# Wider weights, grouped transposes, reordered loads and new priorities in a fused attention and feed-forward kernel

## The chip, the cores and the metric

The kernel runs on one core of one Trainium2 chip. The time is the device time of that core in microseconds (us), lower is better. Each kernel was run several times; a "fast" run is one within 1.5% of the fastest of the same kernel. Engines: PE is TensorE's matmul side, PEld its weight loads, DVE is VectorE, ACT is ScalarE, POOL is GpSimd, SP issues most DMAs.

## The reference, cut to what matters

The input x has 2048 tokens of 448 values. The output is x plus two branches that share one layer norm.

```python
xn = layernorm(x)                                   # S = 2048, D = 448
# branch A: 16 heads of 28; pq = q @ w_phi, pk = k @ w_phi per head
phi_q = concat(softmax(pq), softmax(-pq))           # phi_k likewise: 56 features a head
kv  = einsum("bhsf,bhsd->bhfd", phi_k, v);  z = sum over s of phi_k
o   = einsum(phi_q, kv) / (einsum(phi_q, z) + 1e-6)
A   = o @ wo
# branch B: F = 1792
B   = silu(xn @ w1) @ w2
out = x + A + B
```

All inputs are bf16. 448 is 3.5 times 128, so every product over D has three full blocks of 128 rows and a remainder of 64.

## The kernel before: the parts that matter here

The program is written as a list of operations with their reads and writes. A planner inside the kernel simulates them with estimated durations and so fixes the order of each engine's instructions before anything runs. On the chip each engine then runs its list in that order and waits on semaphores. So an estimate or a priority changes only the order; but a wrong place in the order can stall an engine that has other ready work behind it.

```python
def transpose(dst, src, idn, name):                 # one planned operation for each transpose
    P.op("pe", 56.0, lambda e: e.transpose(dst, src, idn), ...)

def ln_tile(t):                                     # 128 tokens
    ...                                             # DVE statistics, POOL (var + eps) ** -0.5
    P.op("dve", 390, ... xn = (x - mean) * rstd)    # columns 0:448
    P.op("dve", 170, ... xn_sb[:, sl, D:512] = xn_sb[:, sl, KF:D])   # remainder again, KF = 384
    tps = bank16[7][:, 0:512]...                    # one PSUM bank for all x transposes
    for kt in range(4):
        transpose(tps[:, kt, :], xn_sb[:, sl, kt * 128:(kt + 1) * 128], ident[:], "xnT_tr")
    copy(dstx, tps, 512, "xnT_ev")                  # DVE; tiles 8 to 15 are transposed by DMA instead
```

The first layer of branch B (w1, then Silu) works on chunks of 512 tokens, so chunk 1 needs the transposed tiles 4 to 7. `fold` multiplies w_phi into wq and wk: eight weight transposes, an ACT copy, eight small matmuls and a copy, four times.

The attention stage takes 16 tiles; DVE sums, POOL normalises and TensorE accumulates kv:

```python
def kv(t):
    for c in range(CC):                             # CC = 8, KP = 112, DA = 29
        mm(banks[5][0:KP, c*2*DA:(c+1)*2*DA], E_sb[:, sl, 1, c*KP:(c+1)*KP],   # weights 128 x 112
           vaug[:, t % NV, 2*c:2*c+2, :]..., ...)                              # 58 moving columns
```

The second layer of branch B (w2) is TensorE's filler. For the first eight tiles it is kept in SBUF as Y; for the others it stays in PSUM and wo is added to it:

```python
P.cur_prio = 3                                      # larger number: later choice
for t in range(NYT): y_tile(t, [6, 7][t % 2])       # NYT = 8, PSUM banks 6 and 7
...                                                 # order of outputs: 8, 0, 9, 1, ...
b = OUT_BANKS[ob_cnt[0] % 4]                        # 6, 7, 4, 5
q = att(t)                                          # U matmuls, divide, transpose, ACT copy; NQ = 3 buffers
if t < NYT: finish_tile(t, q, b, Y_sb[:, t, :], True)
else:
    P.cur_prio = 2
    ffn2(t, b, False)                               # filler
    P.cur_prio = 0
    finish_tile(t, q, b, x_sb[:, t, :], False)      # wo matmuls, DVE add, store
```

The softmax here doesn't subtract the row's maximum and nothing guards it: scores larger than these inputs give would overflow.

## Time and profile before

| kernel | median us | range | runs |
|---|---|---|---|
| before, with the prediction | 172.46 | 171.56 to 172.88 | 3 |

How to read the numbers below. "Busy" of PE counts from the start of a matmul to its modelled end, so overlapping matmuls hide how much time each really takes. The Trainium skill says so ("Trainium Kernel Development and Optimization", Performance Expectations: matmul busy time "is a bad metric for how close a kernel is to roofline, because matmuls are pipelined"); eight kv matmuls below are busy for 0.55 us but hold PE for 0.39 us. I therefore also use the *slot* of a matmul: the time from its start to the start of the next one, worked out from the trace. In this kernel the usual slot is 216 ns for 512 moving columns, 189 ns for 448 and 56 ns for a 128x128 transpose. Time above the usual slot is a wait of TensorE, but for one thing: the trace has 1170 matmul records for 1176 weight loads, and the slots of double length that the missing records leave are not counted as waits.

From the page of the kernel before: busy time of each engine, and the chain of work that ended last.

```profile
PE 160.1 (94%) x1170; PEld 88.6 (52%) x1176; DVE 92.0 (54%) x179; ACT 85.3 (50%) x135; POOL 68.9 (40%) x82
PEclk9999999999999999999999999999999999999999
PE 81%; DVE 6%; DMA 5%; SPq 3%; POOL 2%; issue 1%; ACT 0%; DVEq 0%
```

TensorE bounds the kernel. The table by stretch (us, then busy time and count of PE, PEld, DVE, ACT, POOL, clock, DMA share, GB/s) for the attention stage:

```profile
63.40:126.00 62.60, 62.60 (x434) 35.90 (x433) 43.97 (x40) 39.69 (x83) 53.12 (x32) 1.00 0.36 61
```

PE has no free time there: its gaps are filled with second-layer matmuls. So work taken from PE in this stretch should shorten the run. How long the kv matmuls hold PE is seen in two places. The table of groups (count, then busy us and mean ns of one, then idle time before):

```profile
L421 PEld LDWEIGHTS psum<-vaug,E_sb 128*112 128x112 bf16 x128 | 9.1, 132 | 2.4
L421 PEld LDWEIGHTS psum<-KVm,phT 112*128 112x128 bf16 x128 | 5.4, 98 | 0.9
```

And the timeline of PE (start, us, engine, line, operation, tiles, shapes, count), one kv group and one group of U matmuls, which also have 58 moving columns:

```profile
74.36 0.55 PE L421 MATMUL psum<-vaug,E_sb 128*112 128x58 bf16 x8
74.75 0.73 PE L421 MATMUL psum<-Wfull,xnT_sb 128*128 128x448 bf16 x3
...
127.98 0.39 PE L421 MATMUL psum<-KVm,phT 112*128 112x58 bf16 x8
128.21 0.54 PE L421 MATMUL psum<-w_sb,hT 128*128 128x448 bf16 x2
```

Read the starts, not the durations: eight kv matmuls hold PE 74.75 - 74.36 = 0.39 us, eight U matmuls 128.21 - 127.98 = 0.23 us. Summed over the trace, the 128 kv matmuls take 6.24 us of slots, the 128 U matmuls 3.70.

PE is not saturated at two places after the start. The timeline of PE between chunk 0 and chunk 1 of the first layer:

```profile
18.79 0.28 PE L433 MATMUL psum<-ident,xn_sb 128*128 128x128 bf16 x2
18.90 3.40 PE L421 MATMUL psum<-xnT_sb,phT 128*128 128x512 bf16 x15
22.13 0.28 PE L433 MATMUL psum<-ident,xn_sb 128*128 128x128 bf16 x2
22.24 1.78 PE L421 MATMUL psum<-xnT_sb,phT 128*128 128x512 bf16 x8
24.42 0.40 PE L433 MATMUL psum<-ident,xn_sb 128*128 128x128 bf16 x4 [0.40 <-DVE xnT_sb L440]
...
25.86 0.40 PE L433 MATMUL psum<-ident,xn_sb 128*128 128x128 bf16 x4 [0.34 <-DVE xnT_sb L440]
26.78 0.40 PE L433 MATMUL psum<-ident,xn_sb 128*128 128x128 bf16 x4 [0.52 <-DVE xnT_sb L440]
27.69 1.47 PE L421 MATMUL psum<-xnT_sb,phT 128*128 128x512 bf16 x6 [0.52 <-DVE xnT_sb L440]
```

Tile 4 is transposed in two halves (18.79 and 22.13), then tiles 5, 6 and 7 follow one at a time, each waiting for DVE to empty the single bank. The second place is in the output stage:

```profile
140.56 1.87 PE L421 MATMUL psum<-w_sb,hT 128*128 128x448 bf16 x9
143.14 0.93 PE L421 MATMUL psum<-wo_sb,oT_sb 112*128 112x448 bf16 x4 [0.72 <-DVE Y_sb L651]
144.76 1.69 PE L421 MATMUL psum<-wo_sb,oT_sb 112*128 112x448 bf16 x8 [0.69 <-ACT oT_sb L436]
```

The last Y tile sits in a bank that the next output tile needs.

### The profile page before, as it was taken

What the parts mean: (1) busy time and instruction counts of PE and PEld (TensorE: products, weight loads), DVE (VectorE), ACT (ScalarE), POOL (GpSimd) and SP (SyncE); (2) the same over time, 40 slices, a digit from 0 to 9 for tenths busy, and PEclk for the clock granted to TensorE, in tenths of its full rate; (3) what the DMA queues carried; (4) which work ended last, traced back from release to release, by engine and by line L of the source; (5) the groups of instructions that cost most, each with busy time, mean ns of one, the idle gap of its engine ahead of it and who ended that gap; (6) DMA issues with size and microseconds to landing.
All of it is one profiled execution on the core that took longest, in us unless ns stands there. A gap on an engine that the chain in (4) does not pass through costs nothing.

```text
span 170.6 us, 2962 instructions
## 1 busy us (share of the span) xinstructions
PE 160.1 (94%) x1170; PEld 88.6 (52%) x1176; DVE 92.0 (54%) x179; ACT 85.3 (50%) x135; POOL 68.9 (40%) x82
## 2 busy tenths in 40 slices
PE   6779986999999999999999999999999996999993
PEld 6653344333334435556566556655567662665551
DVE  2844899400000000799996499539468963775221
ACT  3284573656567658988873884672005101432110
POOL 5712582300000000199999999998950000000000
PEclk9999999999999999999999999999999999999999
DMA  5999957340000000006423651376451200221111
GB/s 155 281 309 379 331 117 94 65 91 0 0 0 4 0 0 0 2 8 59 82 41 65 123 105 24 56 103 127 80 93 34 81 4 0 76 88 50 34 54 54
DMA packets 29773, 13.94 MB, mean 82 GB/s; under 512 B 22272, under 2 KB 29376, under 8 KB 29760
## 3 DMA queue, kind: packets, MB, share of 16 engines
q1 hardware_dynamic: 29296, 13.74, 34.8%
q8 instruction: 9, 0.15, 0.4%
q10 hardware_dynamic: 464, 0.03, 0.2%
q14 instruction: 4, 0.03, 0.1%
HBM read 6.68 MB, written 1.84 MB: 50 GB/s over the span
## 4 chain that ended last, share of the span: by engine, by line
PE 81%; DVE 6%; DMA 5%; SPq 3%; POOL 2%; issue 1%; ACT 0%; DVEq 0%
PE psum L421 79%; DMA x_sb<-in_A_x_dram 5%; SPq L477 3%; PE psum L433 2%; DVE st L529 2%; POOL rstd L533 2%; DVE xn_sb L536 1%; DVE xnT_sb L440 1%; DVE mv L530 1%; DVE xn_sb L538 1%; POOL ve L531 1%; DVE Y_sb L651 0%; DVE out_sb L684 0%; ACT oT_sb L436 0%; DVEq L793 0%
## 5 line engine op out<-in xcount | busy, mean ns | idle before, releaser
L603 DVE TENSOR_REDUCE Ssum<-E_sb 128x64 f32<-128x1792 bf16 x16 | 31.8, 1985 | 42.8 <-ACT E_sb L436 42.8
L421 PE MATMUL psum<-w_sb,hT 128*128 128x448 bf16 x224 | 49.4, 352 | 0.0
L421 PE MATMUL psum<-xnT_sb,phT 128*128 128x512 bf16 (+1 forms) x218 | 44.8, 380 | 2.0 <-DVE xnT_sb L440 1.3
L611 POOL TENSOR_TENSOR E_sb<-E_sb,Rrec 128x896 bf16<-128x896 bf16 x16 | 27.1, 1699 | 41.3 <-DVE Rrec L605 41.3
L436 ACT ACTIVATE hT<-psum 128x1024 bf16<-128x1024 f32 x28 | 28.7, 1024 | 18.1 <-PE psum L421 18.1
L436 ACT ACTIVATE E_sb<-psum 128x448 bf16<-128x448 f32 (+1 forms) x68 | 33.5, 594 | 5.2 <-PE psum L433 3.9
L421 PEld LDWEIGHTS psum<-xnT_sb,phT 128*128 128x128 bf16 (+1 forms) x224 | 17.2, 97 | 27.3 <-issue 6.2
L421 PEld LDWEIGHTS psum<-w_sb,hT 128*128 128x128 bf16 x224 | 20.7, 98 | 17.0
L421 PE MATMUL psum<-Wfull,xnT_sb 128*128 128x448 bf16 x128 | 29.1, 352 | 0.0
L436 ACT ACTIVATE oT_sb<-psum 112x512 bf16<-112x512 bf16 x16 | 9.3, 597 | 38.6 <-PE psum L421 36.8
L627 POOL TENSOR_TENSOR phq<-E_sb,Rrec 128x896 bf16<-128x896 bf16 x16 | 27.0, 1700 | 0.0
L421 PEld LDWEIGHTS psum<-Wfull,xnT_sb 128*128 128x128 bf16 x128 | 12.3, 99 | 10.6
L421 PE MATMUL psum<-wo_sb,oT_sb 112*128 112x448 bf16 x64 | 14.4, 352 | 1.4 <-DVE Y_sb L651 0.7
L421 PE MATMUL psum<-wv_sb,xnT_sb 128*128 128x448 bf16 x64 | 15.2, 352 | 0.0
L436 ACT ACTIVATE vaug<-psum 128x448 bf16<-128x448 f32 x16 | 9.0, 562 | 11.6 <-PE psum L421 11.5
L529 DVE BATCH_NORM_STATS2 st<-x_sb 128x6 f32<-128x448 bf16 x16 | 9.5, 600 | 5.3 <-DMA x_sb<-in_A_x_dram 5.3
L421 PEld LDWEIGHTS psum<-vaug,E_sb 128*112 128x112 bf16 x128 | 9.1, 132 | 2.4
L671 DVE TENSOR_TENSOR o_sb<-psum,rden 128x448 bf16<-128x448 f32 x16 | 9.7, 619 | 0.7 <-PE psum L433 0.3
L421 PEld LDWEIGHTS psum<-wo_sb,oT_sb 112*128 112x128 bf16 x64 | 6.0, 97 | 7.5 <-ACT oT_sb L436 1.7
L533 POOL TENSOR_TENSOR rstd<-ve,neghalf 128x1 f32<-128x1 f32 x16 | 9.3, 583 | 1.3
L684 DVE TENSOR_TENSOR out_sb<-psum,x_sb 128x448 bf16<-128x448 f32 x8 | 5.0, 624 | 8.1 <-PE psum L421 8.1
L605 DVE RECIPROCAL Rrec<-Ssum 128x64 f32<-128x64 f32 x16 | 8.8, 552 | 0.7
(43 smaller groups left out, 110.0 us busy)
## 6 DMA issues: line engine op xcount, KB each, us to landing
out_dram<-out_sb SPq DMA_DIRECT2D x16, 112.0 KB, 1.7
w_sb<-in_B_w_dram SPq DMA_DIRECT2D x1, 1568.0 KB, 14.2
phT<-in_B_w_dram SPq DMA_DIRECT2D x4, 336.0 KB, 6.5
x_sb<-in_A_x_dram SPq DMA_DIRECT2D x3, 448.0 KB, 8.5
Y_sb<-in_A_wqkv_dram SPq DMA_DIRECT2D x3, 224.0 KB, 4.5
x_sb<-in_A_x_dram SPq DMA_DIRECT2D x2, 224.0 KB, 3.1
wo_sb<-in_A_wo_dram SPq DMA_DIRECT2D x1, 392.0 KB, 14.5
wv_sb<-in_A_wqkv_dram SPq DMA_DIRECT2D x1, 336.0 KB, 9.5
```

The source lines that it names most:

```text
L421: r = e.matmul(dst, lhsT, rhs, start=st, stop=sp, skip_group_check=True)
L433: P.op("pe", 56.0, lambda e: e.transpose(dst, src, idn), reads=[src, idn], writes=[dst], name=name)
L436: P.op("act", d_act(n), lambda e: e.activation(dst, src, func, scale=scale), reads=[src], writes=[dst], table=table, name=name, **keys)
L477: P.dma(lambda e: e.dma_start(out=dst, in_=src), n / 340.0, writes=[dst], name=name, eng=eng)
L529: P.op("dve", 590, lambda e: e.bn_stats(st6[:, t, :], xs), reads=[xs], writes=[st6[:, t, :]], name="bnst")
L533: P.op("pool", 570, lambda e: e.tensor_tensor(rstd[:, t:t + 1], ve[:, t:t + 1], neghalf[:], ALU.pow), reads=[ve[:, t:t + 1], neghalf[:]], ...
L603: P.op("dve", 1950, lambda e: e.tensor_reduce(Ssum[:, sl, :], E64, AXL.X, ALU.add), reads=[E64], writes=[Ssum[:, sl, :]], name="Ssum")
L605: P.op("dve", 550, lambda e: e.reciprocal(Rrec[:, sl, :], Ssum[:, sl, :]), reads=[Ssum[:, sl, :]], writes=[Rrec[:, sl, :]], name="Rrec")
L611: P.op("pool", 1700, lambda e: e.tensor_tensor(E3, E3, Rrec[:, sl, 32:64, None].broadcast_to([128, 32, DH]), ALU.mult), reads=[E3, Rrec[:, ...
L627: P.op("pool", 1700, lambda e: e.tensor_tensor(dst, Eq, Rq[:, :, :, None].broadcast_to([128, CC, 4, DH]), ALU.mult), reads=[Eq, Rrec[:, sl ...
L671: P.op("dve", 620, lambda e: e.tensor_tensor(o3, U3[:, :, 0:DH], rden[:, q, :, None].broadcast_to([128, H, DH]), ALU.mult), reads=[U3[:, : ...
L684: P.op("dve", d_dve(D), lambda e: e.tensor_tensor(out_sb[:, osl, :], ob, addend, ALU.add), reads=[ob, addend], writes=[out_sb[:, osl, :]], ...
```

## The change

The intent, as its parts:

1. The remainder is a fourth slice of 128 columns that overlaps the third (columns 320 to 448), so DVE need not copy it. w1 is loaded in that form too; half matmuls use its halves.
2. Loads come in a new order (x tiles 4 to 7 before the last part of w1), and the operations at the head are put in a fixed order.
3. The kv weights are 128 columns wide, reaching 16 columns into the next slice (zeros after the last); the 16 extra output rows are ignored.
4. The transposes of a tile are one planned operation; so are the kv, U and fold matmuls of a group.
5. One more buffer for o (four), padded to 128 columns. A switch for transposing it by DMA is there but off: TensorE transposed it before and still does.
6. The priorities of the Y tiles and of the later second-layer tiles are swapped.

```diff
+    KS = (0, 128, 256, D - 128)
-        w1_sb = phT[:, 0:3, 0:FF]
-        w1r_sb = phT[:, 3, 0:HF]
+        w1_sb = phT[:, 0:4, 0:FF]
+        EW = 2 * D + 16
+        E_sb = sb("E_sb", [128, NE, 2, EW], BF16)
-        NQ = 3
+        NQ = 4
+        wT_sb = hT[0:KP, 0:8, 3 * 512:S]...           # was in E_sb
[...]
-        load_w1(0, 448)
-        load_w1(896, 1344)
-        (two loads of w1r)
-        load_w1(448, 896)
-        load_w1(1344, 1792)
+        load_w1(0, 512)
+        load(w1_sb[:, 3, :], B_w1[D - 128:D, :], "w1r")
+        load_w1(512, 1024)
         load_x(4, 8)
+        load_w1(1024, FF)
[...]
-            P.op("dve", 170, ... xn_sb[:, sl, D:512] = xn_sb[:, sl, KF:D])
+            if t < XN_DMA0: norm(xn_sb[:, sl, 0:D], 0, D, 390)
+            else: two norms, columns 0:384 and 320:448
-            for kt in range(4):
-                transpose(tps[:, kt, :], xn_sb[:, sl, kt * 128:(kt + 1) * 128], ident[:], "xnT_tr")
+            transposes([(tps[:, kt, :], xn_sb[:, sl, KS[kt]:KS[kt] + 128]) for kt in range(4)], f"tr{t}")
[...]
-                mm(banks[5][0:KP, ...], E_sb[:, sl, 1, c * KP:(c + 1) * KP], ...
+            pe_mms([(banks[5][:, ...], E_sb[:, sl, 1, c * KP:c * KP + 128], ...) for c in range(CC)], ...
[...]
+        chain("bnst0 bnag0 bnst1 bnag1 xn0 bnst2 bnag2 xn1 bnst3 bnag3 ev0 xn2 ev1 xn3 ev2 ev3".split())
+        chain("ve0 rstd0 ve1 rstd1 bdphi ve2 rstd2 ve3 rstd3".split())
+        chain("tr0 wT0 tr1 tr2 fold00 fold01 wT1 tr3".split())
[...]
-        P.cur_prio = 3            # Y tiles
+        P.cur_prio = 2
-                P.cur_prio = 2    # second layer of tiles 8 to 15
+                P.cur_prio = 3
```

## The prediction

> **What bounds it now.** TensorE. The page gives PE 160.1 of 170.6 us busy, DVE 54%, ACT 50%, POOL 40%, clock 1.00 throughout; the chain of waits is 81% PE. In the stretch from 63.4 to 126 us PE is busy 62.6 of 62.6 us: its free places there are filled with second-layer matmuls, so any PE work removed should come off the end. PE is not saturated in four places: before the first real matmul (12.1 us); 24.07 to 27.69 us, 1.73 us idle; 142 to 145 us, 1.41 us idle; and the tail after the last matmul (about 2.9 us).
>
> **What the change does, costed.**
> 1. 128-wide kv weights. A load of 128x112 takes 132 ns in the table of groups, one of 112x128 takes 98. More telling is the slot: in the PE timeline eight kv matmuls hold PE 0.39 us until the next group starts, eight U matmuls (same 58 moving columns, 128-wide weights) 0.23 us. The Trainium skill, "TensorE: Matmul & The Clock Gate", section on weight-path perf modes, says fast weight load applies at exactly 128 non-FP32 weights; the trace agrees in direction. 16 tiles x 0.16 us = 2.5 us, all in the saturated stretch. Gain 2.5.
> 2. Transposes issued as groups, overlapping slices, earlier x load. Now tile 4's four transposes are split (18.57 and 21.92 us), its copy ends only at 24.4, and tiles 5 to 7 follow one by one (one PSUM bank), so chunk 1 of the first layer starts at 27.69 although chunk 0 ended at 24.07. The new load order puts 352 KB less ahead of x tiles 4 to 7; at the 280 KB/us seen between their landings (5.1 and 15.1 us) that is 1.2 us earlier. Each of the first eight tiles loses its 181 ns copy. I expect tile 4 and 5 to be transposed whole inside chunk 0, two tiles to remain, chunk 1 near 26.1 us. Still bounded below by the Silu that frees its banks (about 25.2). Gain 1.5.
> 3. Priorities of the Y tiles and the later second-layer tiles swapped. At 142.46 the eviction of the last Y tile holds the bank that the next output tile needs: PE waits 0.7 us for it and 0.7 us for the following output copy. With Y first this wait should go. Gain 1.4.
> 4. Fixed order at the head. The first layer starts when the fourth copy of transposed x ends (12.02 us). My walk through the new order gives 11.5 to 11.9, POOL's reciprocal-root chain (0.57 us each) now pacing. Gain 0.2, uncertain sign.
> 5. Costs: 229 KB more of w1, off the path; two normalisations instead of one plus copy for tiles 8 to 15, under 0.1 us each on an idle DVE. First-layer matmul count is unchanged. Attention output was already transposed on TensorE, so that part changes only padding and one more buffer: nothing.
>
> **Sum.** 172.5 - 2.5 - 1.5 - 1.4 - 0.2 = 166.9; I say 167.0, range 165.0 to 169.4. Chances: faster by over 2% 0.83, within 2% 0.15, slower 0.02.
>
> **What would show it.** kv weight loads near 98 ns and eight kv matmuls in about 0.23 us; POOL-stage PE busy still 100%; chunk 1 of the first layer starting near 26 us; no PE wait on the Y tile near 140 us; first first-layer matmul at 11.5 to 12.2; tail unchanged.
>
> **What would make it wrong.** Each engine's order is fixed beforehand from estimated durations, so a grouped transpose placed before its data are ready stalls PE; the saved kv time could be lost if the filler matmuls run out while POOL (100% busy from 80 to 120 us, 3.4 us a tile) still paces; the fold could be pushed later and block the third block of chunk 1; or new waits in the output stage replace the Y wait.

## The result, and the profile after

| kernel | median us | range | runs | span of the profiled run |
|---|---|---|---|---|
| before | 172.67 | 171.56 to 173.04 | 4 | 170.6 |
| changed | 166.94 | 166.86 to 166.99 | 4 | 165.1 |

The ratio is 0.9678, with a 95% interval of 0.9632 to 0.9724. Ratios here are the mean time of one kernel's fast runs over that of the other's in the same rounds, so not quite the ratio of the medians. The changed kernel is not only faster: its runs lie within 0.13 us of each other, where those of the kernel before span 1.5 us.

From the page of the changed kernel:

```profile
PE 156.8 (95%) x1170; PEld 84.9 (51%) x1176; DVE 91.3 (55%) x171; ACT 84.9 (51%) x135; POOL 69.3 (42%) x84
PE 91%; DVE 4%; DMA 2%; issue 1%; POOL 0%
```

The chain that ended last now runs along PE for 91% instead of 81%. The attention stage, from the table by stretch (same columns as before):

```profile
63.90:122.00 58.10, 58.10 (x415) 30.91 (x414) 43.28 (x39) 39.38 (x83) 49.51 (x30) 1.00 0.31 60
```

It is 100% busy again. The two stretches were cut by hand and hold different numbers of matmuls, so their lengths can not be compared. The stretch of b1 can (an experiment below with the PE order of the kernel before): from the first kv group to the last it takes 47.69 us, in the kernel before 50.24. The group of kv weight loads, and one kv group in the PE timeline:

```profile
L423 PEld LDWEIGHTS psum<-vaug,E_sb 128*128 128x128 bf16 x128 | 5.3, 97 | 3.9 <-POOL E_sb L618 2.6
```

```profile
75.06 0.39 PE L423 MATMUL psum<-vaug,E_sb 128*128 128x58 bf16 x8
75.29 0.54 PE L423 MATMUL psum<-Wfull,xnT_sb 128*128 128x448 bf16 x2
```

The load is 97 ns instead of 132, the group holds PE 0.23 us instead of 0.39. The first line also shows something new: some kv weight loads wait for POOL. The way from chunk 0 to chunk 1:

```profile
18.23 0.39 PE L438 MATMUL psum<-ident,xn_sb 128*128 128x128 bf16 x4
18.46 2.00 PE L423 MATMUL psum<-xnT_sb,phT 128*128 128x512 bf16 x10
...
21.69 0.39 PE L438 MATMUL psum<-ident,xn_sb 128*128 128x128 bf16 x4
21.91 1.78 PE L423 MATMUL psum<-xnT_sb,phT 128*128 128x512 bf16 x8
23.63 0.40 PE L438 MATMUL psum<-ident,xn_sb 128*128 128x128 bf16 x4
...
24.54 0.40 PE L438 MATMUL psum<-ident,xn_sb 128*128 128x128 bf16 x4
25.46 1.47 PE L423 MATMUL psum<-xnT_sb,phT 128*128 128x512 bf16 x6 [0.52 <-DVE xnT_sb L447]
```

Tiles 4 and 5 are transposed whole inside chunk 0; chunk 1 starts at 25.46 instead of 27.69. And the output stage around its last Y tile (DVE starts to copy it out of PSUM, to evict it, at 137.92):

```profile
138.03 1.49 PE L423 MATMUL psum<-w_sb,hT 128*128 128x448 bf16 x7
139.35 0.92 PE L423 MATMUL psum<-wo_sb,oT_sb 112*128 112x448 bf16 x4
140.11 0.35 PE L423 MATMUL psum<-w_sb,hT 128*128 128x448 bf16 x1
```

The last Y tile is still late, but seven filler matmuls stand between its eviction and the output that needs its bank, and PE does not wait.

**Where the 5.5 us of span went.** Sums of PE slots from the first first-layer matmul to the last matmul of all, 154.90 us before and 150.12 after, and the start itself:

| term | before | after | difference |
|---|---|---|---|
| start of the first layer | 12.38 | 11.78 | -0.60 |
| kv matmuls (128 slots) | 6.24 | 3.73 | -2.51 |
| slots just before kv groups, over the usual | 0.01 | 0.31 | +0.30 |
| last Y tile: two long slots | 1.74 | 0 | -1.74 |
| chunk 0 to chunk 1: long slots | 2.35 | 0.69 | -1.66 |
| fold work not yet done when the first layer starts | | | +0.84 |

The last line: before, 24 weight transposes and 16 fold matmuls were done by then, after only 16 and 8. The eight transposes (56 ns) and eight matmuls (49 ns) that moved behind the start are 0.45 + 0.39 = 0.84 us. The sum is -5.4, the span fell by 5.5.

### The profile page after: what moved, and what is told of

Read it like the earlier page. It is cut to its first block, busy times and chain, and to the rows that moved or that the text cites. A ratio compares the mean times of both kernels' runs of the same rounds, so it can differ in the third digit from the quotient of the medians.

```text
span 165.1 us, 2962 instructions
## 1 busy us (share of the span) xinstructions
PE 156.8 (95%) x1170; PEld 84.9 (51%) x1176; DVE 91.3 (55%) x171; ACT 84.9 (51%) x135; POOL 69.3 (42%) x84
## 4 chain that ended last, share of the span: by engine, by line
PE 91%; DVE 4%; DMA 2%; issue 1%; POOL 0%
PE psum L423 87%; PE psum L438 4%; DMA x_sb<-in_A_x_dram 2%; DVE xnT_sb L447 1%; DVE st L533 1%; DVE xn_sb L541 1%; DVE out_sb L695 0%; POOL rstd L538 0%; DVE mv L534 0%; POOL ve L536 0%
## 5 line engine op out<-in xcount | busy, mean ns | idle before, releaser
L610 DVE TENSOR_REDUCE Ssum<-E_sb 128x64 f32<-128x1792 bf16 x16 | 31.6, 1977 | 38.7 <-ACT E_sb L443 38.7
L423 PE MATMUL psum<-w_sb,hT 128*128 128x448 bf16 x224 | 49.9, 352 | 0.0
L443 ACT ACTIVATE hT<-psum 128x1024 bf16<-128x1024 f32 (+1 forms) x32 | 32.8, 1024 | 22.8 <-PE psum L423 18.3
L443 ACT ACTIVATE E_sb<-psum 128x448 bf16<-128x448 f32 x64 | 29.4, 566 | 5.6 <-POOL phq L633 5.2
L423 PEld LDWEIGHTS psum<-Wfull,xnT_sb 128*128 128x128 bf16 x128 | 12.2, 98 | 10.4
L541 DVE TENSOR_SCALAR xn_sb<-x_sb,mv,rstd 128x448 bf16<-128x448 bf16 (+2 forms) x24 | 8.2, 373 | 1.9 <-DMA xnT_sb<-xn_sb 1.6
```

The lines of the kernel that those rows point to most:

```text
L423: r = e.matmul(dst, lhsT, rhs, start=st, stop=sp, skip_group_check=True)
L443: P.op("act", d_act(n), lambda e: e.activation(dst, src, func, scale=scale), reads=[src], writes=[dst], table=table, name=name, **keys)
L541: P.op("dve", dur, lambda e: e.tensor_scalar(dst, x_sb[:, t, c0:c1], mv[:, t, 0:1], rstd[:, t:t + 1], ALU.subtract, ALU.mult), reads=[xs, ...
L610: P.op("dve", 1980, lambda e: e.tensor_reduce(Ssum[:, sl, :].rearrange("p (i h) -> p i h", i=2), E64, AXL.X, ALU.add), reads=[E64], writes ...
```

## The experiments

Names: a kernel whose name begins with a is the changed one with one part undone; b is the kernel before with one part alone; c is other. "Idle" is PE time above the usual slot.

### kv weights: a1_kv112 and b1_kv128

```diff
 # a1, on the changed kernel                                    # the order of every engine stays the same
-E_sb[:, sl, 1, c * KP:c * KP + 128]  -> banks[5][:, ...]
+E_sb[:, sl, 1, c * KP:(c + 1) * KP]  -> banks[5][0:KP, ...]
 # b1, on the kernel before: the reverse, with E_sb 16 columns wider and the folded-weight scratch moved out of it
```

> Changed kernel with only the kv weights cut back to 112 columns; every engine's order is the same as in the changed kernel. Theory (the weight width costs TensorE time in a stretch where it is never free): kv slot 29 to 52 ns for 128 matmuls, 169.3 to 169.6 us against 166.9. Rival (the stretch is paced by POOL, so TensorE time there is free): stays within 0.5 us of 166.9.

> Kernel before with only the kv weights widened to 128 columns, order unchanged. Theory: 2.5 us off, 169.9 to 170.4 us against about 172.6. Rival (POOL paces the stretch, or the saving only opens a wait later because the order is fixed): under 1 us off.

Measured: a1 169.03 (168.97 to 169.11, 4 runs), b1 169.70 (168.85 to 171.18, 4 runs) against 172.93 of the kernel before (ratio of b1 0.9811, 0.9748 to 0.9875). The medians of b1 and the kernel before are 3.2 us apart, but the kernel before read higher in this call than in the others (172.2 to 172.7), so I go by the spans of the profiled runs: a1 167.25 against 165.13 of the changed kernel, b1 167.99 against 170.62. The width alone is worth 2.6 us of span on the kernel before and 2.1 on the changed one. The rival falls. a1 came out 0.3 us below its range, and the trace shows why: the changed kernel loses 0.31 us in the slots before kv groups, a1 3 ns in all. The waits of PEld in the changed kernel (waiter, releaser, us in total, times, longest):

```profile
PEld psum L423 <- POOL E_sb L618: 2.6, 9, 0.4
```

Such a line is missing in a1. With faster kv matmuls PE reaches some groups before POOL has normalised their tile. So POOL takes back about an eighth of the gain. The prediction had feared a loss to POOL for the case that the filler runs out; here filler was left. The waits come only on the changed kernel: a2, a3, a4, c1 and c6 lose 0.25 to 0.31 us in these slots too, b1 and c3 only 3 ns.

### Priorities and the fourth o buffer: a2_prio, b2_prio, b4_nq4

```diff
 # a2, on the changed kernel
-P.cur_prio = 2   (Y tiles)             +P.cur_prio = 3
-P.cur_prio = 3   (later second layer)  +P.cur_prio = 2
 # b2, on the kernel before: the reverse
 # b4, on the kernel before
-NQ = 3
+NQ = 4
```

> Changed kernel with the two priorities swapped back. Theory (the priorities alone decide the wait for the last Y tile): the wait near 142 us comes back, 1.7 us more, about 168.6 us. Rival (the fourth o buffer removed the wait): stays within 0.4 us of 166.9.

> Kernel before with only the two priorities swapped. Theory: the two TensorE gaps near 142 and 144 us (883 and 853 ns over a normal slot) go, 1.7 us off, about 170.9 us. Rival (fourth o buffer needed): within 0.4 us of before.

> Kernel before with four o buffers instead of three. Theory (buffers play no part): within 0.4 us of before. Rival (the fourth buffer removes the wait near 142 us): about 1.7 us faster.

Measured: b2 170.40 (median of the fast runs, 170.29 to 171.09; one slow run of 173.56 left out) against 172.93 (ratio 0.9854, 0.9804 to 0.9904), a2 172.61 (172.57 to 172.76), b4 176.48 (176.21 to 177.24) against 172.16 (mean of six fast runs; one slow run of 174.31 left out). The idle time after 126 us, from the slots:

| kernel | buffers | priorities | idle after 126 us | last Y: eviction starts |
|---|---|---|---|---|
| before | 3 | old | 1.9 | 142.5 |
| b2_prio | 3 | new | 0.1 | 125.1 |
| b4_nq4 | 4 | old | 6.0 | 159.8 |
| a2_prio | 4 | old | 6.0 | 155.3 |
| changed | 4 | new | 0.1 | 137.9 |

The priorities alone remove the wait: 1.8 us of idle time on the kernel before. The buffer alone does not help, and with the old priorities it hurts: b4 is 4.3 us slower than the kernel before, a2 5.7 us slower than the changed one, where I had expected 1.7. For b4 both of my expectations failed. The waits of PE in b4 after 126 us (same columns):

```profile
PE psum L421 <- ACT oT_sb L436: 2.7, 4, 0.8
PE psum L421 <- DVE Y_sb L651: 0.7, 1, 0.7
PE psum L433 <- ACT oT_sb L436: 0.7, 1, 0.7
PE psum L421 <- DVE rden L668: 0.6, 1, 0.6
```

One wait for Y is followed by a row of waits for each tile's own chain of divide, transpose and copy. The last Y is evicted at 159.8, so the outputs that need its bank come at the very end, and there is no filler left to cover their chains: no second-layer matmul starts after it in b4 or in a2, against 56 in the kernel before and 67 in the changed one. That the extra buffer lets the planner use up the filler earlier is my reading of this order, not shown by a run of its own. The effect is shown: both kernels with four buffers and old priorities have it, the other three have not.

### Grouped transposes and the x load: a3_ungroup, b3_group, a4_xlate

```diff
 # a3, on the changed kernel, for tiles 4 to 7
-transposes([four pairs], f"tr{t}")
+for kt in range(4): transposes([one pair], f"tr{t}")
 # b3, on the kernel before: all four transposes of a tile in one planned operation of 224 ns
 # a4, on the changed kernel
-load_x(4, 8); load_w1(1024, FF)
+load_w1(1024, FF); load_x(4, 8)
```

> Changed kernel with the transposes of x tiles 4 to 7 issued one by one again (tiles 0 to 3 stay grouped). Theory (grouping lets a whole tile be transposed at each block boundary): tile 4 is split over two boundaries again, chunk 1 of the first layer starts 1 to 2 us later, 168.0 to 168.9 us. Rival (the earlier x load and the dropped copies do it): within 0.4 us of 166.9.

> Kernel before with only the transposes of each x tile issued as one group. Theory: chunk 1 starts near 26 us instead of 27.7, 1 to 1.7 us off, 171.0 to 171.6 us. Rival (load order or dropped copies): within 0.4 us of before.

> Changed kernel with x tiles 4 to 7 loaded after all of w1, as before. TensorE order is the same. Theory (grouping decides, the load has slack since tile 4 is transposed only at 18.2 us): first statistics of tile 4 about 2 us later, time within 0.4 us of 166.9. Rival (the earlier load is needed): 0.5 to 1.7 us slower.

Measured: a3 167.51 (167.47 to 167.62), b3 172.02 (171.17 to 172.70) against 172.16, a4 166.81 (166.78 to 167.07). Grouping is worth 0.6 us in the changed kernel, less than the 1 to 2 us I had expected, and nothing measurable alone. In a3 chunk 1 starts at 26.10 instead of 25.46, with two long slots (682 ns each over the usual) where the changed kernel has one. In b3 tiles 4 and 5 are transposed whole inside chunk 0, as intended, but DVE has its statistics for later tiles in front: the copy of tile 5 starts at 24.40 and that of tile 6 only at 26.37, one slot there is 1037 ns too long, and chunk 1 starts at 27.75 as before. My theory, that grouping decides, fell for the kernel before.

On the changed kernel the earlier load is worth nothing. In a4 the first statistics of tile 4 start at 14.45 instead of 12.64, and the time stays. PE takes that tile only at its next block boundary, at about 18 us in both.

This does not carry over to the kernel before. The first statistics of tile 4 on DVE, in the kernel before and in the changed one (same columns as for PE):

```profile
15.14 0.63 DVE L529 BATCH_NORM_STATS2 st<-x_sb 128x6 f32<-128x448 bf16 x1 [3.11 <-DMA x_sb<-in_A_x_dram]
...
12.64 0.63 DVE L533 BATCH_NORM_STATS2 st<-x_sb 128x6 f32<-128x448 bf16 x1 [1.14 <-DMA x_sb<-in_A_x_dram]
```

In the kernel before and three others with its DVE order up to there, DVE works from the landing of the load to chunk 1 with no gap over 0.24 us, and chunk 1 follows the landing, not the start of the first layer:

| kernel | first layer starts | first statistics of tile 4 | chunk 1 starts | from statistics to chunk 1 |
|---|---|---|---|---|
| b2 | 12.94 | 14.80 | 27.35 | 12.55 |
| b1 | 12.35 | 15.11 | 27.66 | 12.55 |
| before | 12.38 | 15.14 | 27.69 | 12.55 |
| b4 | 13.57 | 15.99 | 28.54 | 12.55 |
| a4 | 11.61 | 14.45 | 25.30 | 10.85 |
| changed | 11.78 | 12.64 | 25.46 | 12.82 |

In the last two DVE has gaps in which it waits for transposes of PE (0.76 us and less in a4, up to 1.24 us in the changed kernel, before its copy at 18.66), so there the load has slack. a4 therefore shows that the changed kernel can do without the earlier load; it does not show that the load was worth nothing on the way from the kernel before. No run adds the earlier load to that kernel.

### The copy that the overlapping slices save: c6_copy

```diff
 # on the changed kernel, for tiles 0 to 7; nobody reads the result
+P.op("dve", 170, ... xn_sb[:, sl, D:512] = xn_sb[:, sl, KF:D], name=f"xnd{t}")   # and in the fixed order, after each xn
```

> Changed kernel with the remainder copy (181 ns on DVE) put back for x tiles 0 to 7; nothing reads it. Theory (the overlapping slices shorten the DVE chain that feeds the first layer): first layer starts 0.2 to 0.5 us later, chunk 1 up to 0.3 us later, time 0.2 to 0.6 us over 166.9. Rival (DVE has slack there): within 0.15 us.

Measured: 167.00 (166.97 to 167.09, 6 runs), 0.06 above the changed kernel; start of the first layer 11.65. The rival holds: DVE has slack in the changed kernel. The copy that the overlapping slices save is worth nothing in time there. Two things stay untested: nothing reads the copy, so c6 has its DVE time but not the wait of the transposes for it; and no run undoes copy and load together, which may stand in for each other.

### The fixed order at the head: c2_nochain

```diff
 # on the changed kernel
-chain("bnst0 ...");  chain("ve0 ...");  chain("tr0 ...")
```

> Changed kernel without the fixed order at the head; its planner then puts the first eight weight transposes (they wait for a weight load) ahead of the first x transposes on TensorE, as in the kernel before. Theory (in the kernel before, the landing of that load sets the start of the first layer, which its profiles show at 12.35 to 13.57 us): first layer starts at 12.2 us or later, time within 0.8 us of 166.9 but with a spread of over 1 us between executions against 0.15 to 0.3 us for the changed kernel. Rival (the fixed order plays no part, the spread has another cause): spread stays under 0.4 us and the start at 11.6 to 11.8 us.

Measured: 167.11 over all six runs. The profiled execution is not usable: it took 930.24 us (see the last section but one). The five others took 166.62 to 167.43, mean 166.98. So the fixed order does not change the mean, but the spread is 0.8 us against 0.13 of the changed kernel: less than I expected, and clearly more than the rival allows. The start of the first layer could not be read. The order could: in c2 52 warm-up matmuls stand before the weight transposes, not 36 as in the kernel before, so it is not shown that PE waits for the load there.

The other profiles show what differs at the head. In the kernel before, PE's list has 36 warm-up matmuls and then eight weight transposes that wait for a weight load; in the changed one all 56 warm-up matmuls run through and an x transpose comes next. The PE timelines of the kernel before, of b4 (same list at the head) and of the changed kernel:

```profile
1.42 3.89 PE L468 MATMUL psum<-ident 128*128 128x128 bf16 x36 [1.42 <-POOL ones L443]
5.98 0.65 PE L433 MATMUL psum<-ident,Y_sb 128*112 128x128 bf16 x8 [0.67 <-DMA Y_sb<-in_A_wqkv_dram]
```

```profile
1.41 4.02 PE L468 MATMUL psum<-ident 128*128 128x128 bf16 x36 [1.41 <-POOL ones L443]
6.13 1.10 PE L433 MATMUL psum<-ident,Y_sb 128*112 128x128 bf16 x8 [0.69 <-DMA Y_sb<-in_A_wqkv_dram]
```

```profile
1.42 5.09 PE L475 MATMUL psum<-ident 128*128 128x128 bf16 x56 [1.42 <-POOL ones L450]
6.35 0.39 PE L438 MATMUL psum<-ident,xn_sb 128*128 128x128 bf16 x4
```

In b4 the eight transposes take 1.10 us instead of 0.65: TensorE was still at half clock (the slots are 106 to 112 ns before the moment of full clock, 56 after). The clock records of the trace give that moment:

| list at the head | kernels | full clock at | first layer starts at |
|---|---|---|---|
| weight transposes first | before, b1, b2, b3 | 4.5 to 6.0 | 12.35 to 12.94 |
| weight transposes first | b4, c3 | 9.83, 10.65 | 13.57, 13.77 |
| x transposes first, fixed | changed, a1, a2, a3, a4, c6 | 4.1 to 6.8 | 11.61 to 11.78 |

The Trainium skill ("TensorE: Matmul & The Clock Gate", Part 1) says that full clock is granted after a busy window of about 3.4 us, and that the window is free-running, so the moment varies from run to run. The profiles agree with the second: full clock came within a span of 3 us in most. They agree with the first only in part: the stretches at full clock last 46 to 49 times 3.413 us (157.01 to 167.25), but in a4 full clock came 2.7 us after the first matmul. In two of the six kernels with the pause for the load after about 5.3 us it came one window or so later. The six with the fixed order had it in time. Six against six with two exceptions is not a proof that the pause is to blame.

Nor does the head explain the spread of the kernel before. In the table under "Grouped transposes and the x load", b2 starts the first layer 0.59 us after b1 and chunk 1 0.31 us before it; what chunk 1 follows is the landing of x tiles 4 to 7, which moved by 1.2 us over these four profiles. Where the spread of c2 comes from is not known.

### Three parts alone: c3_three

```diff
 # on the kernel before: the edits of b1, b2 and b3 together
```

> Kernel before with three parts of the change at once: 128-wide kv weights, the two priorities swapped, the x transposes grouped; loads, copies, buffers and the order at the head stay as before. Theory (the parts add up, each as measured alone on the kernel before in TensorE time: 2.5, 1.8 and 0.2 us): 4.5 us off, 167.7 to 168.4 us against about 172.5, with no TensorE gap near 140 us; what is left to 166.9 then belongs to the other parts. Rival (each part makes the planner lay out the whole order anew, so parts do not add): outside 167.4 to 168.8 us, with new TensorE gaps of over 0.4 us.

Measured: 167.78 (median of the fast runs, 166.96 to 167.92; one slow run of 170.01 left out), ratio 0.9712 (0.9675 to 0.9750). This is in the range for parts that add up, and no gap near 140 us is left: 0.1 us of idle time after 126 us. Its profiled run is one of those with late full clock; the first layer started at 13.77, 1.4 us later than in the kernel before, and yet chunk 1 started at 27.65 against 27.69. Two different limits give these two numbers. In the kernel before DVE sets chunk 1, as shown above. In c3 the load landed earlier (first statistics of tile 4 at 14.25), DVE waits for transposes of PE (0.46 and 0.60 us), and the long slots of PE sum to 0.69 us as in the changed kernel: here the late start of the first layer sets chunk 1.

Three parts thus give 4.7 of the 5.7 us between the medians, and the fastest run of c3 equals the changed kernel's median. The 0.8 us left belong to the rest of the change together. In the profiled runs they lie before chunk 1: c3 starts it 2.19 us later than the changed kernel and needs 1.18 us less after it, since the 0.84 us of fold work is done by then and the 0.31 us of waits for POOL are absent. The load of x, the copies and the fixed order each cost nothing when undone alone on the changed kernel (a4, c6, c2); that does not rule out that they stand in for one another.

### A further version: c1_head

```diff
 # on the changed kernel
-chain("tr0 wT0 tr1 tr2 fold00 fold01 wT1 tr3".split())
+chain("tr0 wT0 fold00 fold01 tr1 wT1 tr2 tr3 fold10 fold11".split())
```

> Changed kernel with another fixed order on TensorE: the first two fold groups right after the first weight transposes, where TensorE idles at 7.0 to 8.7 us, and the second two before the first layer. Theory (0.84 us of fold and weight transposes is moved into idle time before the first layer, and POOL starts earlier, which takes away the 0.3 us of waits before the kv matmuls): 165.7 to 166.2 us. Rival (filler matmuls already hid it): within 0.3 us of 166.9.

Measured: 166.29 (165.81 to 166.91, 6 runs); c6, the changed kernel with an idle copy, has 167.00 on the same chip. The first layer starts at 11.69 with 24 weight transposes and 16 fold matmuls done, so the 0.84 us of work did move into idle time and most of it was gained. But the time missed its range by 0.1, since the second half of the expectation failed: the waits for POOL before kv groups are unchanged (0.31 us). This version is the fastest of all, by 0.65 us over the changed kernel, and pays with spread: its runs span 1.1 us. Its fold matmuls stand ahead of the second x tile's transposes, so what the weight load does may again be passed on to the head; that this makes the spread is not shown.

## Why the prediction was right, point by point

The time (167.0 predicted, 166.94 measured) and the main mechanism, that TensorE work and TensorE waits come off the end one for one, were right. Terms of the sum:

- **kv weights: 2.5 predicted.** The slots gave 2.51, a net 2.2 after 0.3 of new waits for POOL (2.1 of span in a1), 2.6 alone on the kernel before. The mechanism is shown by a1, whose order is the same as the changed kernel's. The Trainium skill's rule ("TensorE: Matmul & The Clock Gate", weight-path perf modes: the fast load applies at 128 weights that are not FP32) agrees with 97 against 132 ns.
- **Chunk 0 to chunk 1: 1.5 predicted.** The start moved from 27.69 to 25.46, by 2.23 instead of the predicted 1.6, and the long slots lost 1.66. The term is mis-sized, since 0.84 us of fold work came behind the start of the first layer: net 0.8. (That is a matter of booking: it could stand against the head. c1 does this work first and starts at 11.69 all the same.) The reasons "earlier x load" and "loses its 181 ns copy" are not borne out on the changed kernel, where undoing one of them costs 0 (a4) or 0.06 (c6). On the kernel before, the single PSUM bank was not the limit that the prediction took it for: DVE was busy from the landing of the load to chunk 1 for all but 0.9 of 12.5 us, which fits that grouping alone (b3) gained nothing. "Transposes issued as groups" is right for 0.6 of it in the changed kernel and for nothing on the kernel before.
- **Priorities: 1.4 predicted.** 1.74 measured; I had counted the idle time of the profile (1.41), which takes a matmul as busy to its modelled end, rather than the slots. The cause was named rightly: b2 shows it alone.
- **Head: 0.2 predicted, sign uncertain.** The start came 0.60 earlier, inside the predicted 11.5 to 12.2. c2 shows no change of the mean without the fixed order. I did not foresee the change of the spread.
- **"One more buffer: nothing."** Right only with the new priorities. With the old ones it costs 4.3 us (b4); a2 has the same 6.0 us of idle time. I had costed the parts as if each could be put in or left out alone.

Measured terms: 2.2 + 0.8 + 1.74 + 0.6 = 5.3 against 5.6 predicted and 5.5 of span. The total was as good as it was because the errors of the terms nearly cancel, and that is luck.

What stays open: how the remaining parts share the move of chunk 1's start from the 27.4 to 28.5 of the kernels with the old load order to 26.1 (a3), and the 0.8 us between c3 and the changed kernel. The load landed 2.5 us earlier (first statistics of tile 4 at 12.64 instead of 15.14), and the copies are gone from DVE; but no run has both undone, or the load alone on the kernel before. Further candidates not run alone are the new estimates of the loads in the planner, the order of the statistics on DVE, the moved scratch and the split norms.

## What to carry to other kernels

On an engine that is never free, count slots (start to start), not busy time: 20 ns a slot on 128 small matmuls was the largest single gain, and "100% busy" looked the same before and after. In a kernel whose engines run in a fixed order, parts of a change interact: a harmless extra buffer cost 4 us under the wrong priorities, so undo parts from the new kernel and try them on the old one, and expect the two to differ. A part that costs nothing when undone from the new kernel may still have counted on the old one: x could land 1.8 us later in a4 without loss, while in the kernel before chunk 1 followed its landing.

## One execution set aside

The profiled execution of c2 took 928.4 us of span, against 164.8 to 165.5 for its five other runs. The group of its second-layer matmuls in that profile:

```profile
L423 PE MATMUL psum<-w_sb,hT 128*128 128x448 bf16 x224 | 275.5, 1534 | 0.0
L610 DVE TENSOR_REDUCE Ssum<-E_sb 128x64 f32<-128x1792 bf16 x16 | 32.2, 2014 | 392.3 <-ACT E_sb L443 392.3
```

A matmul of 448 columns took 1534 ns instead of 352, its slot 1075 instead of 189, while DVE was as fast as ever (2014 against 1977 ns for its reduction). The mean clock reads 1.00, but this trace holds no clock record at all, where each of the other profiles has one of full clock from 4.1 to 10.7 us on; without records the reading is 1.00 whatever the clock. The result was correct. No cause is known, and no other of the runs shows it.

## What the Trainium skill lacked or had wrong

- "TensorE: Matmul & The Clock Gate", weight-path perf modes: it gives a trigger for the fast load and about 40 ns for small FP8 matmuls, but no bf16 slot with the fast load and without. Here, with 58 moving columns: 29 ns a matmul with 128 weight columns, 49 ns (6.24 us over 128) with 112.
- The same page, back-to-back issue gap: its sustained figures of about 81 ns at N=128 and 131 ns at N=512 are not seen. Transposes of 128 columns with a weight load each ran at 56 ns a slot, matmuls of 512 columns at 216.
- The same page, Part 1: it calls a ramp penalty under 1% of a typical span and advises not to fit it. Here full clock came at 4.1 to 6.8 us in eleven profiles and at 9.8 and 10.7 in two, and kernels with the second case started their main work up to 1.4 us later. That is 0.8% of the span, so the bound holds, but parts of this change were worth less than that.
- The same page, HAM trace caveats: it reports the clock stuck at a quarter for over 50 us. Here one whole execution of 928 us ran at 1075 ns a slot instead of 189 (5.7 times), without any clock record; what the page lacks is that a profile without records then reads as a clock of 1.00.
- "Trainium Kernel Development and Optimization", Performance Expectations, names MFU and the weight-load busy share as the good metrics. Here the weight-load share fell from 52% to 51% while 5.5 us went, so it did not show the gain; the slots did.
